# Attention and soft MoE in one kernel: V loaded as 32 keys per partition and turned by VectorE, weights in 8 KB rows with all experts on chip, second layer in four column groups

## The chip, the cores and the metric

The kernel runs on one core of one Trainium2 chip. The metric is device time in microseconds (us). The span of a profiled execution differs from the timed median by a few us (239.4 against 235.39 for the kernel before); stages are read from the span. The runs of a kernel spread over about 3% here, and comparisons use the fast runs. The profiled execution of the kernel before was one of its slower ones: the spans of its fast runs in later calls are 232.2 to 237.4 us. So a difference of some 3 us between its stages and those of another profile says little.

The views of the profile name the engines: PE is TensorE's matmuls, PEld its weight loads, DVE is VectorE, ACT is ScalarE, POOL is GpSimd, and SP issues DMAs. "L294" is line 294 of the kernel. The granted clock is the share of TensorE's full clock that it was allowed, 1.00 at most. The chain is the work that ended last, followed back step by step to what released it.

## The reference

Eight batches of eight heads, 576 queries and keys each, head size 64; 16 "beacon" keys per head come first and are visible to every query, the 576 others are causal. The attention output is the input `x` (4608 x 512) of a soft mixture of experts with 8 experts of 4 slots.

```python
k_all = concatenate([beacon_k, k], axis=2)            # 16 + 576 keys
v_all = concatenate([beacon_v, v], axis=2)
scores = where(causal, -1e9, q @ k_all.T / 8)
attn = softmax(scores) @ v_all                        # B,H,S,D -> x: (B*S, H*D)
logits = x @ phi                                      # 4608 x 32
slot_input = softmax(logits, axis=0).T @ x            # 32 x 512
h = relu(slot_input[e] @ w1[e]); slot_out[e] = h @ w2[e]   # 512x1024, 1024x512
out = softmax(logits, axis=1) @ slot_out
```

## The kernel before

The kernel works through 32 pairs of heads, four pairs per batch. `n` is the pair, `g = n % 4` its place in the batch. In each pair TensorE computes scores of pair `n`, transposes q and k of pair `n + 1`, and multiplies the exponentials of pair `n - 1` with V. A batch's routing (transposes of `x`, logits, their transposes `dT`, slot inputs) is spread as pieces of work over the next batch's pairs. In the timelines below each engine takes its own instructions in program order.

V is read as rows of 64 float32 (256 bytes), one key per partition, and cast by GpSimd and VectorE:

```python
    def load_v(b, part):
        for c in ((0, 1), (2,), (3,), (4,))[part]:
            vf[(b, c)] = vfp.tile([P, H, D], FP, name="vf", tag="vf")
            if c == 0:
                nc.sync.dma_start(out=vf[(b, c)][0:Nb], in_=beacon_v[b].rearrange("h n d -> n h d"))
            lo, hi = max(0, c * P - Nb), min(S, (c + 1) * P - Nb)
            p0 = lo + Nb - c * P
            nc.sync.dma_start(out=vf[(b, c)][p0:p0 + hi - lo],
                              in_=v[b, :, lo:hi, :].rearrange("h p d -> p h d"))
# ... cut ...
    def cast_v(b, c):
        kn = P if c < 4 else UL
        (nc.vector if c % 2 else nc.gpsimd).tensor_copy(out=vh[b % 2][0:kn, c, :, 0:D], in_=vf[(b, c)][0:kn])
```

The slot inputs of a batch need the transposed logits `dT`, which VectorE copies out of PSUM, the memory that TensorE writes to:

```python
    def dt_piece(b):
        # ... cut: five TensorE transposes of eLh into tp ...
        nc.vector.tensor_copy(out=dT[b][:, 0:4, :], in_=tp[:, 0:4, :])
        nc.vector.tensor_copy(out=dT[b][0:UL, 4, :], in_=tp[0:UL, 4, :])
        nc.vector.memset(dT[b][0:Nb, 0, :], 0.0)
    # si_piece(b): TensorE multiplies x with dT[b]
    for n in range(NP + 1):                       # the loop over pairs, shortened
        score(n, 0); (0, 2, 3, 2)[n % 4] pieces of routing work; score(n, 1)
        transp(n + 1); attend(n - 1, 0); score(n, 2); attend(n - 1, 1); score(n, 3)
        load_pair(n + 5); load_v(b + 1, g); cast_v(...); now and then load_w(...)
```

In the third pair of a batch (g = 2) the work is the last transpose and both logits pieces; in the fourth (g = 3) it is `dt_piece` and `si_piece`. The experts' weights are cast to float16 by GpSimd's DMA in 1 MB pieces (source rows of 4 KB for w1 and 2 KB for w2) into six rotating buffers per matrix; experts 6 and 7 wait until a buffer is free. The MoE stage then runs, expert by expert:

```python
        nc.scalar.activation(hTz[:, e, :, e * SPE:(e + 1) * SPE], hp[:, :, :], AF.Relu)
        for t in range(NFC):                                         # 8 matmuls, one after the other
            nc.tensor.matmul(sop[0:NSL, :], hTz[:, e, t, :], w2h[e][:, t * Dm:(t + 1) * Dm],
                             start=(e == 0 and t == 0), stop=(e == E - 1 and t == NFC - 1))
```

The softmax here doesn't subtract the row's maximum and nothing guards it: scores larger than these inputs give would overflow.

## Time and profile before

| | us |
|---|---|
| Median of the 3 runs | 235.39 (235.05 to 239.95) |
| Profiled span | 239.4 |
| Routing sums begin (end of attention and its routing) | 180.24 |
| Routing sums and MoE stage, to the scaling of the slot outputs | 30.96 (180.24 to 211.20) |
| Output stage | 28.2 (211.20 to 239.4) |

From the page of the kernel before: busy time and its share of the span with the number of instructions, then the busy tenths in 40 slices of 6 us. PEclk is the clock that TensorE was granted, in tenths.

```profile
PE 187.1 (78%) x3512; PEld 129.1 (54%) x3512; DVE 130.8 (55%) x304; ACT 127.4 (53%) x187; POOL 89.4 (37%) x161
...
PE   0579778869986898797898698899869999979800
...
PEclk9999889985999799999999979689996569995555
DMA  6999999999899899999999999272599999919995
...
q1 hardware_dynamic: 50880, 38.35, 56.3%
q0 software_dynamic: 12800, 16.78, 41.5%
```

DMA is full in attention and again while the last weights come in. The two last lines are the DMA queues: packets, MB written, share of 16 engines. Of q1, the records of single packets give 54.0 us of all 16 engines to packets of 256 bytes, nearly all of them V.

Busy time by window, kernel before: window, its length, busy us of PE, PEld, DVE, ACT and POOL with instruction counts, granted clock, DMA share (over 1 where packets overlap), GB/s written.

```profile
100.00:120.00 20.00, 17.48 (x419) 13.00 (x417) 14.53 (x35) 14.74 (x22) 10.79 (x18) 1.00 1.17 262
180.00:190.00 10.00, 9.43 (x124) 5.15 (x121) 1.35 (x7) 0.40 (x2) 4.30 (x6) 0.59 1.18 205
```

TensorE is busy 17.48 of 20 us in attention, with DMA saturated as well. In the MoE stage it runs at a granted clock of 0.59, while the DMA engines are full with the last experts' weights.

The timeline of one fourth pair of the kernel before (start, duration, engine, line, what; in brackets idle time before and its releaser):

```profile
108.35 0.49 DVE L237 TENSOR_TENSOR xb_141<-av_153,r_2528 128x320 f16<-128x320 f32 x1
...
109.07 0.23 DVE L285 COPY dT<-tr 128x128 f16<-128x128 f16 x1 [0.23 <-PE tr L283]
...
109.35 0.07 DVE L287 MEMSET dT<- 16x16 uint32 x1
109.48 0.67 PE L294 MATMUL tr<-dT,xb_142 128*128 128x32 f16 x20 [0.45 <-DVE dT L287]
```

VectorE finishes the third pair at 108.84 and is free when the logits' transposes arrive; TensorE loses 0.45 us before the slot inputs (L294).

The second layer before, two experts of the chain of work that ended last (start, duration, what):

```profile
187.56 3.59 PE av_152 L397 x8
...
196.97 1.90 PE av_152 L397 x8
```

### The profile page before, as it was taken

Reading aid. Unit: us, or ns where it says so; the run is one execution under the profiler, and the core shown is the slowest. Engines: PE = TensorE matmul, PEld = TensorE weight load, DVE = VectorE, ACT = ScalarE, POOL = GpSimd, SP = SyncE. Lnnn points to the kernel's source line nnn. Section 1 sums busy time; section 2 is a strip of 40 time slices with the busy share of each in tenths; the row PEclk is TensorE's granted clock in tenths of the full one; section 3 lists DMA queues with packets and bytes.
Section 4 is the critical chain, followed back from the end, with each engine's and each line's share of the span. In section 5 each row is a group of like instructions: output and inputs, shape, how many; then the busy total and the mean of one; then the engine's idle time right before and its main releaser. Section 6 shows DMA issues by size and latency. Waiting matters only on the chain.

```text
span 239.4 us, 8048 instructions
## 1 busy us (share of the span) xinstructions
PE 187.1 (78%) x3512; PEld 129.1 (54%) x3512; DVE 130.8 (55%) x304; ACT 127.4 (53%) x187; POOL 89.4 (37%) x161
## 2 busy tenths in 40 slices
PE   0579778869986898797898698899869999979800
PEld 0457566647664766575666476677646445532200
DVE  4583967555777566777667666566652000058800
ACT  2075576747767487776786758477710000057700
POOL 4080645442652732744645363443542420000000
PEclk9999889985999799999999979689996569995555
DMA  6999999999899899999999999272599999919995
GB/s 193 225 300 281 317 225 243 298 258 240 220 248 228 193 230 282 205 273 263 258 317 262 230 201 277 43 127 41 92 161 202 209 206 210 159 81 422 416 413 248
DMA packets 63715, 55.63 MB, mean 232 GB/s; under 512 B 41920, under 2 KB 50112, under 8 KB 62656
## 3 DMA queue, kind: packets, MB, share of 16 engines
q1 hardware_dynamic: 50880, 38.35, 56.3%
q0 software_dynamic: 12800, 16.78, 41.5%
q8 instruction: 27, 0.44, 0.8%
q14 instruction: 8, 0.07, 0.1%
HBM read 62.46 MB, written 9.44 MB: 300 GB/s over the span
## 4 chain that ended last, share of the span: by engine, by line
PE 47%; DMA 16%; ACT 13%; DVE 5%; SPq 5%; POOL 5%; issue 4%; ACTq 0%
DMA vf<-in_v_dram 14%; ACT ex L208 10%; PE av_152 L397 8%; PE sc_156 L202 6%; PE av_152 L229 6%; PE tr L187 6%; PE fp L413 5%; PE tr L256 3%; DVE xT L261 3%; PE tr L392 3%; PE sc_157 L202 3%; SPq L103 3%; PE tr L271 2%; PE av_153 L229 2%; DMA kf<-in_k_dram 2%
## 5 line engine op out<-in xcount | busy, mean ns | idle before, releaser
L208 ACT ACTIVATE ex<-sc_156 128x1024 f16<-128x1024 f32 x64 | 63.0, 984 | 47.4 <-PE sc_156 L202 47.2
L208 ACT ACTIVATE ex<-sc_157 128x992 f16<-128x992 f32 x64 | 48.0, 751 | 12.2 <-PE sc_157 L202 12.1
L210 POOL TENSOR_SCALAR_AFFINE_SELECT ex<-ex 128x1024 f16<-128x1024 f16 x32 | 34.9, 1092 | 46.9 <-ACT ex L208 46.9
L229 PEld LDWEIGHTS <-ex 128*128 128x128 f16 (+2 forms) x960 | 40.6, 113 | 12.8 <-issue 10.9
L397 PE MATMUL av_152<-w2h,hTz 128*32 128x512 f16 x64 | 20.1, 471 | 2.3 <-ACT hTz L395 2.3
L187 PE MATMUL tr<-idb,kf 64*64 64x64 bf16 x576 | 16.6, 204 | 2.0 <-issue 0.8
L261 DVE COPY xT<-tr 128x1024 f16<-128x1024 f16 x16 | 10.5, 687 | 13.2 <-PE tr L256 13.2
L187 PEld LDWEIGHTS <-qf 64*64 64x64 bf16 x576 | 13.4, 118 | 7.4 <-issue 6.2
L187 PE MATMUL tr<-idb,qf 64*64 64x64 bf16 x576 | 16.8, 205 | 0.6 <-DMA qf<-in_q_dram 0.5
L395 ACT ACTIVATE hTz<-tr 128x32 f16<-128x32 f32 x8 | 1.6, 198 | 28.8 <-PE tr L392 28.8
L401 DVE TENSOR_SCALAR soh<-av_152,rd 32x512 f16<-32x512 f32 x1 | 0.7, 737 | 29.0 <-PE av_152 L397 29.0
L187 PEld LDWEIGHTS <-kf 64*64 64x64 bf16 x576 | 14.3, 119 | 2.9 <-issue 2.6
L413 PE MATMUL fp<-soh,eLh 32*128 32x512 f16 x36 | 14.1, 522 | 1.4 <-DVE soh L401 0.8
L415 ACT ACTIVATE osb<-fp,rc 128x512 f32<-128x512 f32 x18 | 11.8, 687 | 5.9 <-PE fp L413 5.6
L202 PE MATMUL sc_156<-qT_129,kT_132 64*128 64x128 bf16 (+1 forms) x110 | 9.6, 276 | 6.9 <-POOL kT_132 L192 4.8
L243 POOL CAST vh_138<-vf 128x512 f16<-128x512 f32 (+1 forms) x12 | 7.7, 639 | 19.0 <-DMA vf<-in_v_dram 19.0
L216 POOL TENSOR_SCALAR_AFFINE_SELECT ex<-ex 80x160 f16<-80x160 f16 x32 | 10.6, 331 | 10.7 <-ACT ex L208 10.3
L202 PEld LDWEIGHTS <-kT_132 64*128 64x128 bf16 (+1 forms) x198 | 8.6, 110 | 11.1 <-POOL kT_132 L192 5.7
L417 DVE TENSOR_SCALAR osb<-fp,rc 128x512 f32<-128x512 f32 x18 | 13.1, 748 | 2.4 <-PE fp L413 1.6
L120 POOL DMA_DIRECT2D w1h<-in_moe_w_dram x16 | 11.5, 724 | 6.6 <-PE tr L392 6.6
L120 POOL DMA_DIRECT2D w2h<-in_moe_w_dram x16 | 12.1, 758 | 4.4 <-PE av_152 L397 4.4
L229 PE MATMUL av_153<-vh_138,ex 128*128 128x65 f16 (+2 forms) x240 | 11.5, 202 | 2.1 <-issue 2.1
(206 smaller groups left out, 318.9 us busy)
## 6 DMA issues: line engine op xcount, KB each, us to landing
qf<-in_q_dram SPq DMA_DIRECT2D x32, 288.0 KB, 6.2
kf<-in_k_dram SPq DMA_DIRECT2D x32, 288.0 KB, 6.3
w1h<-in_moe_w_dram POOLq DMA_DIRECT2D x16, 512.0 KB, 8.6
w2h<-in_moe_w_dram POOLq DMA_DIRECT2D x16, 512.0 KB, 8.9
out_dram<-osb SPq DMA_DIRECT2D x8, 1024.0 KB, 8.2
vf<-in_v_dram SPq DMA_DIRECT2D x24, 256.0 KB, 7.0
vf<-in_v_dram SPq DMA_DIRECT2D x8, 224.0 KB, 6.9
vf<-in_v_dram SPq DMA_DIRECT2D x8, 160.0 KB, 7.2
```

The lines of the kernel that those rows point to most:

```text
L120: nc.gpsimd.dma_start(out=d[e][:, o:o + 2048].rearrange("p (c f) -> p c f", c=c), in_=src)
L187: nc.tensor.transpose(tp[po:po + 64, j, :], hi, idb[po:po + 64, po:po + 64])
L202: nc.tensor.matmul(sc[0:kn, a, col:col + un], kT[n % 3][64 * a:64 * a + 64, P * c:P * c + kn], qT[n % 3][64 * a:64 * a + 64, u0:u0 + un], ...
L208: nc.scalar.activation(ex[n][:, :, o:o + w], sc[:, :, 0:w], AF.Exp, scale=scale)
L210: nc.gpsimd.affine_select(out=ex[n][:, :, 0:512].rearrange("p a (c t) -> p a c t", c=4), in_=ex[n][:, :, 0:512].rearrange("p a (c t) -> p ...
L216: nc.gpsimd.affine_select(out=ex[n][0:UL, :, o:o + UL], in_=ex[n][0:UL, :, o:o + UL], compare_op=AL.is_ge, fill=0.0, base=0, pattern=[[0, ...
L229: nc.tensor.matmul(avs[a][0:m, i * DD:(i + 1) * DD], ex[n][0:kn, a, o:o + m], vh[b % 2][0:kn, c, h, :], start=(c == 0), stop=(c == i))
L261: nc.vector.tensor_copy(out=xT[b][:, :, P * cs[0]:P * cs[0] + 2 * P].rearrange("p t (i u) -> p i t u", i=2), in_=tp[:, :, :, :])
L397: nc.tensor.matmul(sop[0:NSL, :], hTz[:, e, t, :], w2h[e][:, t * Dm:(t + 1) * Dm], start=(e == 0 and t == 0), stop=(e == E - 1 and t == NF ...
L413: nc.tensor.matmul(fp_[:, :], etok(cg, j), soh[:, :], start=True, stop=True)
L415: nc.scalar.activation(osb[:, j, :], fp_[:, :], AF.Copy, scale=rc[:, i:i + 1])
L417: nc.vector.tensor_scalar(out=osb[:, j, :], in0=fp_[:, :], scalar1=rc[:, i:i + 1], scalar2=None, op0=AL.mult)
```

## The change

Its intent: fewer and larger DMA packets, so that DMA no longer limits attention; no casts of V; the MoE stage without waits for weights and with a shorter second layer. Space for all experts is found by lending the last two experts' place to the q, k and V buffers during attention. The core of the diff, with cuts marked by dots and three comments put in for cut code:

```diff
+    TK = 32
...
+        # 32 keys of one head on a partition (8 KB source row), cast to float16 by GpSimd's DMA
+            nc.gpsimd.dma_start(
+                out=main[32 * qd:32 * qd + 32, :],
+                in_=bass.AP(tensor=v.tensor, offset=v.offset + b * H * S * D + lo,
+                            ap=[[S * D, H], [4 * TK * D, 4], [1, TK * D]]))
...
+        # rest(m): keys 496 to 575, one row per head
+        for what in (((0, 1), (16,)), ((2, 3), ()), ((), (17, 18)), ((), ()))[part]:
+            for x in what:
+                (block if x < 16 else rest)(x)
+    def turn_v(b, tail):
+        src = vtile(b, tail).bitcast(FP).rearrange("p (j e) -> p e j", j=TK)
+        dst = vh[b % 2].bitcast(FP)
+        if tail:
+            nc.vector.transpose(
+                out=dst[0:96, 0:4].rearrange("p c h e -> p e (c h)")[:, 0:D // 2], in_=src[0:96])
+        else:
+            nc.vector.transpose(
+                out=dst[:, 1:NCH].rearrange("p c h e -> p e h c")[:, 0:D // 2], in_=src)
...
+    # beacon_v_in(b): beacon rows by GpSimd's DMA into vh, after the transposes
...
-            src = moe_w1[e, r * 256:(r + 1) * 256].rearrange("(c p) f -> p c f", p=P)
+            src = moe_w1[e, r * 256:(r + 1) * 256].rearrange("(p r) f -> p (r f)", r=2)
...
-        nc.gpsimd.tensor_copy(out=kT[n % 3][:, 0:Nb], in_=bkT[:, n, :])
+        nc.vector.tensor_copy(out=kT[n % 3][:, 0:Nb], in_=bkT[:, n, :])
...
             if b + 1 < B:
                 load_v(b + 1, g)
-                for c in ((), (0, 1), (2,), (3, 4))[g]:
-                    cast_v(b + 1, c)
+                if g == 2:
+                    turn_v(b + 1, 1)
+                    turn_v(b + 1, 0)
+                if g == 3:
+                    beacon_v_in(b + 1)
-            if n % 3 != 2 and n >= 3 and wl < 24:
+            want = 23 * (n + 1) // 28 if n < 28 else (25, 28, 30, 32)[n - 28]
+            while wl < want:
...
+            z = 32 * (t % 4)
+            nc.tensor.matmul(sop[z:z + NSL, :], hTz[:, e, t, :], w2c(e, t),
+                             start=(e == 0 and t < 4), stop=(e == E - 1 and t >= 4))
+    for e in range(E + 1):
+        if e < E:
+            first_layer(e)
+        if e > 0:
+            second_layer(e - 1)
```

Cut: the layouts of first-layer weights (read with a step of four elements) and slot inputs that go with it, and the fourfold copy of routing weights and logits, so that the last matmul adds the four groups.

More of the change, by code (lines that the diff above doesn't have):

```diff
@@ L46 @@
     DD = D + 1
+    DP = D + 2
     scale = 1.0 / D ** 0.5
@@ L70 @@
     const = ctx.enter_context(tc.tile_pool(name="const", bufs=1))
-    qkp = ctx.enter_context(tc.tile_pool(name="qkp", bufs=5))
-    vfp = ctx.enter_context(tc.tile_pool(name="vfp", bufs=6))
     exq = ctx.enter_context(tc.tile_pool(name="exq", bufs=2))
     sml = ctx.enter_context(tc.tile_pool(name="sml", bufs=4))
-    wh = ctx.enter_context(tc.tile_pool(name="wh", bufs=6))
+    arena = const.tile([P, E * 8192], F16, name="arena")
+    lend = (E - 2) * 8192
     sc_scope = ExitStack()
@@ L82 @@
     qf, kf = {}, {}
+    QKS = 5
     def load_pair(n):
         b, g = divmod(n, H // 2)
-        for (d, src, nm) in ((qf, q, "qf"), (kf, k, "kf")):
-            t = qkp.tile([P, J, D], FP, name=nm, tag=nm)
+        for i, (d, src) in enumerate(((qf, q), (kf, k))):
+            o = lend + (2 * (n % QKS) + i) * 2 * J * D
+            t = arena[:, o:o + 2 * J * D].bitcast(FP).rearrange("p (j d) -> p j d", j=J)
             nc.sync.dma_start(
-                out=t[:, :, :],
+                out=t,
                 in_=src[b, 2 * g:2 * g + 2].rearrange("h s d -> (h s) d").rearrange(
@@ L92, in load_pair @@
             d[n] = t
-    vf = {}
-    def load_v(b, part):
-        for c in ((0, 1), (2,), (3,), (4,))[part]:
-            vf[(b, c)] = vfp.tile([P, H, D], FP, name="vf", tag="vf")
-            if c == 0:
-                nc.sync.dma_start(out=vf[(b, c)][0:Nb], in_=beacon_v[b].rearrange("h n d -> n h d"))
-            lo, hi = max(0, c * P - Nb), min(S, (c + 1) * P - Nb)
-            p0 = lo + Nb - c * P
-            nc.sync.dma_start(out=vf[(b, c)][p0:p0 + hi - lo],
-                              in_=v[b, :, lo:hi, :].rearrange("h p d -> p h d"))
+    TK = 32
@@ new lines, with vtile, block, rest @@
+    vend = lend + 2 * QKS * 2 * J * D
+    vmore = const.tile([P, 2, TK * D], F16, name="vmore")
+    def vtile(b, tail):
+        if b % 2 == 0:
+            return vmore[:, tail, :]
+        return arena[:, vend + tail * TK * D:vend + (tail + 1) * TK * D]
+    vrows = v.rearrange("b h s d -> (b h) (s d)")
+    vall = v.rearrange("b h s d -> (b h s d)")
+    vh = [const.tile([P, NCH, H, DP], F16, name=f"vh{i}") for i in range(2)]
+    def load_v(b, part):
+        main, tail = vtile(b, 0), vtile(b, 1)
+        def block(qd):
+            lo = (32 * qd - Nb) * D
+            if b == 0 and qd == 0:
+                nc.gpsimd.dma_start(out=main[0:1, Nb * D:TK * D], in_=vrows[0:1, 0:(TK - Nb) * D])
+                nc.gpsimd.dma_start(
+                    out=main[1:4, :],
+                    in_=bass.AP(tensor=v.tensor, offset=v.offset + lo + 4 * TK * D,
+                                ap=[[4 * TK * D, 3], [1, TK * D]]))
+                nc.gpsimd.dma_start(
+                    out=main[4:32, :],
+                    in_=bass.AP(tensor=v.tensor, offset=v.offset + S * D + lo,
+                                ap=[[S * D, H - 1], [4 * TK * D, 4], [1, TK * D]]))
+                return
+            nc.gpsimd.dma_start(
+                out=main[32 * qd:32 * qd + 32, :],
+                in_=bass.AP(tensor=v.tensor, offset=v.offset + b * H * S * D + lo,
+                            ap=[[S * D, H], [4 * TK * D, 4], [1, TK * D]]))
+        def rest(m):
+            lo = (TK * m - Nb) * D
+            w = min(TK * D, S * D - lo)
+            p0 = 32 * (m - 16)
+            nc.gpsimd.dma_start(out=tail[p0:p0 + H, 0:w],
+                                in_=vrows[b * H:(b + 1) * H, lo:lo + w])
+        for what in (((0, 1), (16,)), ((2, 3), ()), ((), (17, 18)), ((), ()))[part]:
+            for x in what:
+                (block if x < 16 else rest)(x)
@@ new lines, in turn_v, with beacon_v_in @@
+    def turn_v(b, tail):
[3 more added lines that the diff above has]
+            nc.vector.transpose(
+                out=dst[0:96, 0:4].rearrange("p c h e -> p e (c h)")[:, 0:D // 2],
+                in_=src[0:96])
+        else:
+            nc.vector.transpose(
+                out=dst[:, 1:NCH].rearrange("p c h e -> p e h c")[:, 0:D // 2], in_=src)
+    def beacon_v_in(b):
+        nc.gpsimd.dma_start(out=vh[b % 2][0:Nb, 1, :, 0:D],
+                            in_=beacon_v[b].rearrange("h n d -> n h d"))
@@ L106 @@
     NPC = 4 * E
-    w1h, w2h = {}, {}
+    WP = 2048
+    wloc = [m * WP for m in range(24)] + [lend + WP * x for x in (3, 4, 5, 6, 7, 0, 1, 2)]
     def load_w(m):
         e, r = divmod(m, 4)
-        d, nm = (w1h, "w1h") if r < 2 else (w2h, "w2h")
-        if r % 2 == 0:
-            d[e] = wh.tile([P, 4096], F16, name=nm, tag=nm)
-        o = (r % 2) * 2048
         if r < 2:
-            src = moe_w1[e, r * 256:(r + 1) * 256].rearrange("(c p) f -> p c f", p=P)
+            src = moe_w1[e, r * 256:(r + 1) * 256].rearrange("(p r) f -> p (r f)", r=2)
@@ L117, in load_w, with w1c @@
         else:
-            src = moe_w2[e, (r - 2) * 512:(r - 1) * 512].rearrange("(c p) f -> p c f", p=P)
-        c = src.shape[1]
-        nc.gpsimd.dma_start(
-            out=d[e][:, o:o + 2048].rearrange("p (c f) -> p c f", c=c), in_=src)
+            src = moe_w2[e, (r - 2) * 512:(r - 1) * 512].rearrange("(p r) d -> p (r d)", r=4)
+        nc.gpsimd.dma_start(out=arena[:, wloc[m]:wloc[m] + WP], in_=src)
+    def w1c(e, c, t):
+        o = wloc[4 * e + c // 2] + (c % 2) * F + (t // 4) * 512
+        return arena[:, o:o + 512].rearrange("p (f r) -> p f r", r=4)[:, :, t % 4]
@@ L123, with w2c @@
+    def w2c(e, t):
+        o = wloc[4 * e + 2 + t // 4] + (t % 4) * Dm
+        return arena[:, o:o + Dm]
     load_pair(0)
@@ L126 @@
     load_pair(1)
-    for part in range(4):
-        load_v(0, part)
     phif = const.tile([P, NDC, NSL], FP, name="phif")
@@ L133 @@
     load_pair(4)
+    nc.vector.memset(vtile(0, 0)[0:1, 0:Nb * D], 0.0)
+    nc.vector.memset(vtile(0, 1), 0.0)
+    for part in range(4):
+        load_v(0, part)
+    nc.vector.memset(vtile(1, 1), 0.0)
     idb = const.tile([P, P], BF, name="idb")
@@ L145 @@
         nc.vector.memset(qT[i][:, 0:Nb], 0.0)
-    vh = [const.tile([P, NCH, H, DD], F16, name=f"vh{i}") for i in range(2)]
     for i in range(2):
@@ L149 @@
     xb = [const.tile([P, NCH, H, D], F16, name=f"xb{i}") for i in range(2)]
-    eLh = const.tile([NSL, Nb + N], F16, name="eLh")
+    eLh = const.tile([P, Nb + N], F16, name="eLh")
     nc.vector.memset(eLh[:, 0:Nb], 0.0)
-    dsum9 = const.tile([NSL, 2 * B], FP, name="dsum9")
+    dsum9 = const.tile([P, 2 * B], FP, name="dsum9")
     siacc = const.tile([P, NDC, NSL], FP, name="siacc")
     nc.vector.memset(siacc[:, :, :], 0.0)
-    hTz = const.tile([P, E, NFC, NSL], F16, name="hTz")
-    nc.gpsimd.memset(hTz[:, :, :, :], 0.0)
-    phih = const.tile([P, NDC, NSL], F16, name="phih")
+    phih = const.tile([P, NDC, 4, NSL], F16, name="phih")
     bkT = const.tile([P, NP, Nb], BF, name="bkT")
@@ L231, in attend @@
                     ex[n][0:kn, a, o:o + m],
-                    vh[b % 2][0:kn, c, h, :],
+                    vh[b % 2][0:kn, (c + 1) % NCH, h, 0:DD],
                     start=(c == 0), stop=(c == i))
@@ L239, in attend @@
             in1=r5[:, :].unsqueeze(2).broadcast_to([P, NCH, D]), op=AL.mult)
-    def cast_v(b, c):
-        kn = P if c < 4 else UL
-        (nc.vector if c % 2 else nc.gpsimd).tensor_copy(out=vh[b % 2][0:kn, c, :, 0:D], in_=vf[(b, c)][0:kn])
     xT = {}
@@ L270, in logit_piece @@
         for t in range(NDC):
-            nc.tensor.matmul(lp[0:NSL, 0:w], phih[:, t, :],
+            nc.tensor.matmul(lp[:, 0:w], phih[:, t, :, :].rearrange("p g s -> p (g s)"),
                              xT[b][:, t, Nb + hf * w:Nb + (hf + 1) * w],
@@ L274, in logit_piece @@
         o = Nb + b * S + hf * w
-        nc.scalar.activation(eLh[:, o:o + w], lp[0:NSL, 0:w], AF.Exp,
+        nc.scalar.activation(eLh[:, o:o + w], lp[:, 0:w], AF.Exp,
                              accum_out=dsum9[:, 2 * b + hf:2 * b + hf + 1])
@@ L282, in dt_piece @@
             m = P if i < 4 else UL
-            nc.tensor.transpose(tp[0:m, i, :], eLh[:, b * S + P * i:b * S + P * i + m],
+            nc.tensor.transpose(tp[0:m, i, :], eLh[0:NSL, b * S + P * i:b * S + P * i + m],
                                 idh[0:NSL, 0:NSL])
@@ L295, in si_piece @@
                     sp[:, t, :],
-                    xb[b % 2][0:m, i, 2 * t:2 * t + 2, :].rearrange("p h d -> p (h d)"),
+                    xb[b % 2][0:m, i, 4 * (t // 2):4 * (t // 2) + 4, :].rearrange(
+                        "p h d -> p (h d)").rearrange("p (f r) -> p f r", r=2)[:, :, t % 2],
                     dT[b][0:m, i, :], start=(i == 0), stop=(i == NCH - 1))
@@ L323 @@
         if n == 0:
-            for c in range(NCH):
-                cast_v(0, c)
-            nc.vector.tensor_copy(out=phih[:, :, :], in_=phif[:, :, :])
+            turn_v(0, 1)
+            turn_v(0, 0)
+            beacon_v_in(0)
+            nc.vector.tensor_copy(out=phih[:, :, :, :],
+                                  in_=phif[:, :, :].unsqueeze(2).broadcast_to([P, NDC, 4, NSL]))
         if n >= 1:
@@ L345 @@
                 load_v(b + 1, g)
-                for c in ((), (0, 1), (2,), (3, 4))[g]:
-                    cast_v(b + 1, c)
-            if n % 3 != 2 and n >= 3 and wl < 24:
+                if g == 2:
[5 more added lines that the diff above has]
+            while wl < want:
                 load_w(wl)
                 wl += 1
-    dsum = const.tile([NSL, 1], FP, name="dsum")
-    rd = const.tile([NSL, 1], FP, name="rd")
+    hTz = exq.tile([P, E, NFC, NSL], F16, name="hTz", tag="ex")
+    nc.gpsimd.memset(hTz[:, :, :, :], 0.0)
+    dsum = const.tile([P, 1], FP, name="dsum")
+    rd = const.tile([P, 1], FP, name="rd")
     nc.vector.reduce_sum(out=dsum[:, :], in_=dsum9[:, :], axis=mybir.AxisListType.X)
@@ L372 @@
             i = cg * G + j
-            nc.tensor.matmul(csp[:, i:i + 1], etok(cg, j), ones[0:NSL, :],
+            nc.tensor.matmul(csp[:, i:i + 1], etok(cg, j)[0:NSL], ones[0:NSL, :],
                              start=True, stop=True)
@@ L380, with first_layer @@
     sop = avs[0]
-    while wl < min(NPC, 24):
-        load_w(wl)
-        wl += 1
-    for e in range(E):
-        while wl < min(NPC, 4 * (e + 6)):
-            load_w(wl)
-            wl += 1
+    def first_layer(e):
         hp = ps_tr.tile([P, NFC, SPE], FP, name="tr", tag="tr")
@@ L391, with second_layer @@
             for c in range(NDC):
-                nc.tensor.matmul(hp[:, t, :], w1h[e][:, c * F + t * P:c * F + (t + 1) * P],
-                                 siT[:, c, e * SPE:(e + 1) * SPE],
+                nc.tensor.matmul(hp[:, t, :], w1c(e, c, t), siT[:, c, e * SPE:(e + 1) * SPE],
                                  start=(c == 0), stop=(c == NDC - 1))
         nc.scalar.activation(hTz[:, e, :, e * SPE:(e + 1) * SPE], hp[:, :, :], AF.Relu)
+    def second_layer(e):
         for t in range(NFC):
-            nc.tensor.matmul(sop[0:NSL, :], hTz[:, e, t, :],
-                             w2h[e][:, t * Dm:(t + 1) * Dm],
-                             start=(e == 0 and t == 0), stop=(e == E - 1 and t == NFC - 1))
-    soh = const.tile([NSL, Dm], F16, name="soh")
-    nc.vector.tensor_scalar(out=soh[:, :], in0=sop[0:NSL, :], scalar1=rd[:, 0:1],
+            z = 32 * (t % 4)
[6 more added lines that the diff above has]
+            second_layer(e - 1)
+    soh = const.tile([P, Dm], F16, name="soh")
+    nc.vector.tensor_scalar(out=soh[:, :], in0=sop[:, :], scalar1=rd[:, 0:1],
                             scalar2=None, op0=AL.mult)
@@ L407 @@
     for cg in range(NG):
-        osb = wh.tile([P, G, Dm], FP, name="osb", tag="w1h")
+        osb = arena[:, cg * 4096:(cg + 1) * 4096].bitcast(FP).rearrange("p (j d) -> p j d", j=G)
         dst = out[cg * P * G:(cg + 1) * P * G, :].rearrange("(p j) d -> p j d", j=G)
```

## The prediction

> **What bounds the kernel now.** Three stages, read from the busy times by window and the chain of waits (profiled span 239.4 us).
>
> 1. Attention, 15 to 173 us, 32 head pairs. PE is busy 16 to 17.5 of each 20 us, DMA is saturated (share 0.96 to 1.17). The undisturbed stretch from 99.9 to 118.9 us takes 19.05 us per batch of four pairs; the average is about 20.5. So waits for V (the chain gives 14% to "DMA vf") cost only about 11 us in all. By packet records, V's 256-byte packets take 54 us of all 16 engines, the weights 99.
> 2. MoE, 181.5 to 211.2 us = 29.7 us: first layer 0.93 us per expert, an idle wait for the ReLU, then eight second-layer matmuls, 3.6 us at the halved clock (four experts) or 1.9 us (four).
> 3. Output, 28 us, DMA at over 400 GB/s; unchanged.
>
> **What the change moves.**
>
> - V: 8 KB source rows. Weight packets (2048 source bytes 98 ns, 4096 bytes 172 ns) extrapolate to an estimated 320 ns for 8192: V falls from 54 to about 23 us of DMA time, weights from 99 to about 82. DMA stops being the limit of attention. Worth at most 11 us.
> - VectorE gains two transposes per batch of 1024 four-byte elements. The SBUF cast of 512 float32 took 0.51 to 0.57 us, so an estimated 1.1 us each, and loses two casts.
> - These transposes stand in VectorE's order directly before the dT copies for which TensorE waits in the next pair. Their last two V pieces are issued by GpSimd only in the same pair. Laid over today's timeline: GpSimd would be free at 107.2, two issues of 0.7 us end at 108.6; the Trainium skill ("DMA: Bandwidth & Descriptors", anatomy of one DMA) gives about 2 us fixed cost. VectorE arrives at 108.9, so it waits about 2 us, then transposes for 2.2. TensorE's slot-input matmuls, now at 109.5, would start at about 113: 3.5 to 4.5 us of idle TensorE per batch, seven times = 25 to 31 us, plus some re-throttled clock after each gap, 3 to 8 us.
> - Start: the identity matrix is made after nine GpSimd DMA issues, and batch 0's beacon DMA waits for the transposes: first attention-times-V about 3 us later than 17.6.
> - MoE: four column groups. The skill ("TensorE: Matmul & The Clock Gate", packing small matmuls) gives 2.4 times for three groups, which no run here shows yet. Estimated second layer 0.6 to 1.2 us per expert. The first layer, with stride-4 weights, at most 1.15 us (the stride-4 loads of eLh ran at 36 ns each against 29). The ReLU wait is hidden. Estimated stage 13 to 18 us instead of 29.7: about -14.
>
> **Sum.** Attention -11 + 20 to 35, start +3, MoE -14: from about -2 to +13. I lean to the low side since the stall depends on landing times I cannot see: **240 us, 8 in 10 between 225 and 253; faster by over 2% 0.29, within 2% 0.28, slower 0.43.**
>
> **What would show it.** Right: VectorE waiting for V DMA before the large transposes, once per batch; TensorE idle before the slot-input matmuls on the dT memset or copies; V packets of 8 KB source; DMA share under 1 in attention; MoE about 15 us. Wrong: batches of 19 us without such a gap; MoE still near 30 us; transposes far from 1.1 us.
>
> **What would make it wrong.** If the last V pieces land before VectorE arrives, the stall shrinks to about 2 us per batch and the kernel lands near 225. If strided weight loads or mode switches are slow, MoE gains less.

## The result, and the profile after

| | before | after |
|---|---|---|
| Median, us | 237.67 (4 runs) | 280.14 (4 runs, 278.44 to 281.52) |
| Profiled span, us | 239.4 | 279.5 |
| Routing sums begin, us | 180.24 | 233.15 |
| Routing sums and MoE stage, us | 30.96 | 18.19 (to 251.34) |
| Output stage, us | 28.2 | 28.2 |
| Ratio of fast runs | | 1.1906 (95%: 1.1769 to 1.2044) |

A ratio is the mean time of one kernel's fast runs over that of the other's fast runs of the same rounds, so it is not quite the ratio of the medians quoted. The change makes the kernel 19% slower. MoE gains 12.8 us; attention loses 52.9 us.

From the page of the kernel after, the same lines:

```profile
PE 179.5 (64%) x3512; PEld 129.3 (46%) x3512; DVE 156.8 (56%) x339; ACT 127.4 (46%) x187; POOL 100.5 (36%) x171
...
PE   0647639719941997099619950995099878998800
...
PEclk9999958968985589569957995799558996556985
DMA  7997949937993399469927991699347996005997
```

TensorE now has a hole in every batch, its clock falls to half around each, and DMA, which was to be relieved, swings between full and idle.

Waits of the kernel after (engine and line, for whom; total us, times, longest):

```profile
PE tr L342 <- DVE dT L335: 52.4, 8, 9.5
DVE vh L145 <- DMA arena<-in_v_dram: 18.0, 4, 5.1
DVE vh L145 <- DMA vmore<-in_v_dram: 12.7, 3, 5.4
PE av L282 <- DMA vh<-in_beacon_v_dram: 4.5, 1, 4.5
```

The timeline of the same spot, kernel after, in another batch:

```profile
108.14 1.06 POOL L134 DMA_DIRECT2D vmore<-in_v_dram  x2
...
109.34 0.49 DVE L290 TENSOR_TENSOR xb<-av,r 128x320 f16<-128x320 f32 x1
...
114.08 2.02 DVE L145 STREAM_TRANSPOSE vh<-vmore 96x1024 f32<-96x1024 f32 x1 [4.24 <-DMA vmore<-in_v_dram]
116.13 2.06 DVE L149 STREAM_TRANSPOSE vh<-vmore 128x1024 f32<-128x1024 f32 x1
118.05 0.20 DVE L333 COPY dT<-tr 128x128 f16<-128x128 f16 x1
...
118.44 0.71 PE L342 MATMUL tr<-dT,xb 128*128 128x32 f16 x20 [8.43 <-DVE dT L335]
```

Read from above: GpSimd issues the last two V pieces at 108.14. VectorE arrives at about 109.8, waits 4.24 us, transposes for 4.1 us, and only then copies the `dT` for which TensorE has stood still 8.43 us. TensorE does nothing else in the hole: its next instruction in program order is the one that waits.

The price in clock and what DMA does meanwhile, busy time by window around an earlier hole, kernel after (columns as before):

```profile
70.00:80.00 10.00, 9.21 (x196) 6.76 (x196) 7.25 (x18) 7.23 (x12) 7.74 (x14) 1.00 1.02 235
80.00:90.00 10.00, 1.00 (x27) 0.80 (x27) 4.74 (x6) 1.57 (x3) 1.12 (x2) 0.61 0.68 162
90.00:100.00 10.00, 9.82 (x181) 7.63 (x178) 5.70 (x15) 5.54 (x7) 4.42 (x8) 0.54 0.48 126
```

After the hole TensorE is busy 9.82 of 10 us for 181 matmuls, where 196 had taken 9.21 us, at a granted clock of 0.54 instead of 1.00.

The second layer after, two pieces of the chain:

```profile
238.79 0.97 PE av L450 x8
239.76 1.16 PE tr L443 x32
```

Eight second-layer matmuls take 0.97 us instead of 3.59, both at about half clock, and the ReLU wait between the layers is gone.

### The profile page after: what moved, and what is told of

Its sections match the earlier page's. It is cut to its first block, busy times and chain, and to the rows that moved or that the text cites. A ratio compares the mean times of both kernels' runs of the same rounds, so it can differ in the third digit from the quotient of the medians.

```text
span 279.5 us, 8018 instructions
## 1 busy us (share of the span) xinstructions
PE 179.5 (64%) x3512; PEld 129.3 (46%) x3512; DVE 156.8 (56%) x339; ACT 127.4 (46%) x187; POOL 100.5 (36%) x171
## 4 chain that ended last, share of the span: by engine, by line
PE 37%; DVE 22%; DMA 15%; ACT 14%; POOL 5%; issue 2%; ACTq 0%; DVEq 0%; POOLq 0%
ACT ex L261 12%; PE av L282 9%; PE sc L255 9%; DMA arena<-in_v_dram 6%; PE tr L240 6%; DVE vh L149 6%; DMA vmore<-in_v_dram 6%; DVE vh L145 5%; DVE xT L309 4%; DVE arena L475 3%; PE tr L443 3%; PE av L450 3%; DMA arena<-in_moe_w_dram 2%; ACT eLh L323 2%; PE tr L342 2%
## 5 line engine op out<-in xcount | busy, mean ns | idle before, releaser
L261 ACT ACTIVATE ex<-sc 128x1024 f16<-128x1024 f32 (+3 forms) x128 | 107.1, 869 | 112.5 <-PE sc L255 112.3
L255 PE MATMUL sc<-qT,kT 64*128 64x128 bf16 (+5 forms) x576 | 50.7, 275 | 14.8 <-ACT ex L261 7.0
L282 PE MATMUL av<-vh,ex 128*128 128x65 f16 (+2 forms) x960 | 50.1, 211 | 5.0 <-DMA vh<-in_beacon_v_dram 4.5
L282 PEld LDWEIGHTS <-ex 128*128 128x128 f16 (+2 forms) x960 | 42.5, 117 | 15.2 <-issue 13.3
L342 PE MATMUL tr<-dT,xb 128*128 128x32 f16 (+1 forms) x160 | 5.7, 187 | 52.4 <-DVE dT L335 52.4
L242 DVE COPY qT<-tr 128x576 bf16<-128x576 bf16 x32 | 24.2, 756 | 26.1 <-PE tr L240 26.1
L255 PEld LDWEIGHTS <-kT 64*128 64x128 bf16 (+1 forms) x576 | 22.0, 108 | 25.8 <-issue 12.7
L290 DVE TENSOR_TENSOR xb<-av,r 128x320 f16<-128x320 f32 x64 | 31.4, 491 | 2.2
L240 PE MATMUL tr<-idb,arena 64*64 64x64 bf16 x1152 | 31.8, 212 | 1.3 <-DVE bkT L227 0.4
L240 PEld LDWEIGHTS <-arena 64*64 64x64 bf16 x1152 | 27.5, 126 | 9.6 <-issue 8.7
L242 DVE COPY kT<-tr 128x576 bf16<-128x576 bf16 x32 | 23.9, 746 | 0.1
L166 POOL DMA_DIRECT2D arena<-in_moe_w_dram x32 | 18.2, 568 | 0.3 <-issue 0.3
L145 DVE STREAM_TRANSPOSE vh<-vmore 96x1024 f32<-96x1024 f32 x4 | 8.1, 2024 | 12.7 <-DMA vmore<-in_v_dram 12.7
L475 DVE TENSOR_SCALAR arena<-fp,rc 128x512 f32<-128x512 f32 x18 | 12.7, 747 | 1.5 <-PE fp L471 1.1
```

The source lines that it names most:

```text
L145: nc.vector.transpose(out=dst[0:96, 0:4].rearrange("p c h e -> p e (c h)")[:, 0:D // 2], in_=src[0:96])
L166: nc.gpsimd.dma_start(out=arena[:, wloc[m]:wloc[m] + WP], in_=src)
L240: nc.tensor.transpose(tp[po:po + 64, j, :], hi, idb[po:po + 64, po:po + 64])
L242: nc.vector.tensor_copy(out=dst[:, Nb:Nb + S].rearrange("p (s j) -> p s j", j=J), in_=tp[:, :, :].rearrange("p j s -> p s j"))
L255: nc.tensor.matmul(sc[0:kn, a, col:col + un], kT[n % 3][64 * a:64 * a + 64, P * c:P * c + kn], qT[n % 3][64 * a:64 * a + 64, u0:u0 + un], ...
L261: nc.scalar.activation(ex[n][:, :, o:o + w], sc[:, :, 0:w], AF.Exp, scale=scale)
```

## The experiments

Theory A: VectorE, executing in order, stands at the transposes until V pieces issued in the same pair have landed, then transposes for 4 us, while TensorE waits for `dT`. Rivals: the V transfers themselves are slow or DMA is short (B); clock, GpSimd issues or DMA are causes of their own (C); the paced weights and lent buffers cost attention (D). Times are medians; the medians of the kernel before in the same calls lay between 237.06 and 238.52 us for all timed pairs below.

### v_early: the last V pieces one pair earlier

```diff
-        for what in (((0, 1), (16,)), ((2, 3), ()), ((), (17, 18)), ((), ()))[part]:
+        for what in (((0, 1), (16,)), ((2, 3), (17, 18)), ((), ()), ((), ()))[part]:
```

> Only change to the changed kernel: the last two V pieces of a batch are issued one pair earlier, beside the third and fourth block. Theory A (VectorE, in order, sits on the transposes until the pieces issued in the same pair land, 30.7 us over seven batches in the profile after): VectorE's wait for V falls under 6 us, TensorE's idle time before the slot-input matmuls from 52 us to 25 to 30 us (the two transposes of 2.04 us each stay in the way), time 245 to 256 us. Rival B (the V transfers with 8 KB rows are slow in themselves or DMA is short, so the wait moves to another piece): wait stays above 20 us, time above 270 us.

Measured: 258.91 us, correct, ratio to the kernel before 1.0868. VectorE's wait for V is 7.6 us in all (4.4 and 3.2), TensorE's gap before the slot inputs 33.3 us. Both lie a little above what was expected, and so does the time, but the order of size is that of A, and B is out: the wait does not move elsewhere. What is left of the gap is mostly the transposes themselves (seven times 4.1 us are 28.7).

```profile
PE tr L342 <- DVE dT L335: 33.3, 8, 6.4
```

### late_turn: the transposes one pair later, after the dT copies

```diff
+        if g == 3 and b + 1 < B:
+            turn_v(b + 1, 1)
+            turn_v(b + 1, 0)
         if n + 1 < NP:
             transp(n + 1)
...
-                if g == 2:
-                    turn_v(b + 1, 1)
-                    turn_v(b + 1, 0)
```

> Loads as in the changed kernel, but the two transposes stand one pair later in VectorE's order: after the dT copies and before the copies of q and k. Theory A: the pieces have landed by then (wait under 4 us in all), and about 1 us of the 4.1 us per batch hides while TensorE transposes q; TensorE's gap of 52 us before the slot-input matmuls goes to under 5 us, a new one of about 3 us per batch stands at the scores or the transposes of q and k; time 238 to 252 us. Rival B: no better than v_early by more than noise because 4.1 us of VectorE per batch cost the same wherever they stand.

Measured: 259.33 us, correct, ratio 1.0926: no better than v_early, as the rival said. The gap before the slot inputs fell to 3.6 us, but 31.4 us of waits of the next scores for VectorE took its place. VectorE still waited 16.8 us for V where under 4 were expected, and the time lies above the expected range: a miss for A in this run. It does not show that the place is indifferent: the wait for V is 9.2 us longer than in v_early, so place and wait changed together. A later place without a wait was not run here; fixed2_place below tests the place alone.

### no_turn: no transposes after batch 0 (wrong result)

```diff
                 if g == 2:
-                    turn_v(b + 1, 1)
-                    turn_v(b + 1, 0)
+                    pass
```

(The second V buffer is filled once with a constant.)

> Wrong result on purpose: all V transfers stay, but only batch 0 is transposed; the other batches use what lies in the tiles. Shows what the transposes and their wait cost together. Theory A: TensorE's gaps before the slot-input matmuls fall from 52 us to under 5 us, the clock is granted near full in attention, time 212 to 226 us. Rival C (the throttled clock, the DMA or the GpSimd issues are a cause of their own): above 235 us.

Measured: 218.78 us, result wrong as intended, ratio 0.9192. From its page:

```profile
PE 165.1 (77%) x3512; PEld 118.0 (55%) x3512; DVE 130.8 (61%) x326; ACT 126.9 (59%) x187; POOL 100.4 (47%) x171
...
PEclk9999999999999999999999999999999855579955
DMA  6998699999999999999999999999999900069996
```

The gap before the slot inputs, as long as in the kernel before (3.6 us there too):

```profile
PE tr L342 <- DVE dT L335: 3.6, 8, 0.4
```

All V and weight transfers and all GpSimd issues are still there, so rival C as a cause of its own falls. It also splits the loss. Against this run the profile after is 65.2 us longer (279.5 - 214.3). The gaps before the slot inputs account for 48.8 us of that (52.4 - 3.6), and the same 3512 matmuls are busy 14.4 us longer (179.5 - 165.1), which is the lower clock after the holes. Both together are 63.2 us. A batch of four pairs takes 18.15 us here (five periods between the copies of `x`'s transposes at 57.42 and 148.17 us), 20.5 before and 28.0 after. DMA is as full here as in the kernel before (share 1.05 against 1.07 between 60 and 140 us), so the runs do not show that DMA stopped limiting attention.

### undo_v: V as before, the rest of the change kept

The edit puts `load_v` and `cast_v` of the kernel before in place of the new V path, and nothing else. Its core:

```diff
-                if g == 2:
-                    turn_v(b + 1, 1)
-                    turn_v(b + 1, 0)
-                if g == 3:
-                    beacon_v_in(b + 1)
+                for c in ((), (0, 1), (2,), (3, 4))[g]:
+                    cast_v(b + 1, c)
```

> The changed kernel with the V path of the kernel before (256-byte rows, casts on GpSimd and VectorE), all else kept: 8 KB weight rows, all experts on chip, column groups. Theory A (the V path alone makes the change slow, the rest gains about 13 us in the MoE stage): time 218 to 229 us, MoE stage about 17 us against 29.7. Rival D (the paced weights or the lent buffers cost attention too): above 235 us.

Measured: 233.05 us, correct, ratio 0.9813 (0.9741 to 0.9884): less gain than expected. The MoE stage is as short as in the change, but attention ends later (first-layer loads begin at 186.2 us against 181.5 before), and GpSimd waits 70.2 us for V (28.5 before).

```profile
POOL vh L247 <- DMA vf<-in_v_dram: 70.2, 18, 7.3
```

So rival D has a part here. The likely reason is that all 32 weight pieces now move during attention, beside 256-byte V packets that already filled the DMA engines; pacing and lent buffers were not tested apart. The V path is what makes the change slow; without it the rest gains about 2%.

### m_turn: what a transpose costs

A row of VectorE transposes of scratch data at the end of the kernel before, with other engines idle.

```diff
+    for _ in range(3):
+        nc.vector.transpose(out=c3, in_=a3)     # packed in, packed out
+    for _ in range(3):
+        nc.vector.transpose(out=c3, in_=as3)    # step of 128 bytes in, packed out
+    for _ in range(3):
+        nc.vector.transpose(out=o4, in_=a3)     # packed in, the kernel's step out
+    for _ in range(3):
+        nc.vector.transpose(out=o4, in_=as3)    # both, as the kernel does
```

> The kernel before with a row of VectorE transposes of scratch data at its very end, when GpSimd and the other engines are idle; only their durations matter. In the changed kernel one transpose of 1024 four-byte elements took 2.04 us, not the 1.1 us forecast. Theory W (a four-byte element takes two passes whatever the layout): 1024 float32 with packed input and output still 2.0 to 2.1 us, half of it 1.0 to 1.1 us, 1024 float16 about 1.1 us, 2048 float16 about 2.1 to 2.2 us. Rival S (the strides of input or output cost the time): packed float32 about 1.1 us, and one of the strided forms 2 us. Rival G (GpSimd in the way): all forms 1.1 us here.

Groups of its profile (busy us, mean ns of one, idle before), in the order strided out, strided both, strided in, packed, packed 1024 float16, and last a plain copy with the strided input:

```profile
L444 DVE STREAM_TRANSPOSE tbw<-taw 128x1024 f32<-128x1024 f32 x3 | 6.0, 1997 | 0.1
L446 DVE STREAM_TRANSPOSE tbw<-taw 128x1024 f32<-128x1024 f32 x3 | 6.2, 2064 | 0.1
L442 DVE STREAM_TRANSPOSE tcw<-taw 128x1024 f32<-128x1024 f32 x3 | 5.7, 1905 | 0.1
L440 DVE STREAM_TRANSPOSE tcw<-taw 128x1024 f32<-128x1024 f32 x3 | 3.7, 1245 | 0.1
L448 DVE STREAM_TRANSPOSE tcw<-taw 128x1024 f16<-128x1024 f16 x3 | 3.7, 1232 | 0.1
L452 DVE COPY tcw<-taw 128x1024 f32<-128x1024 f32 x3 | 3.1, 1032 | 0.1
```

Rival S wins, and G is out, since both steps cost 2.06 us with GpSimd idle too. Packed, 1024 four-byte elements take 1.245 us, as long as two-byte ones (1.232). A step on either side makes it 1.9 to 2.0 us, on both 2.06. A plain copy with the same strided input took 1.03 us, so on the input side it is the transpose that minds the step, not VectorE's reads as such; a copy with a strided output was not run. The forecast of 1.1 us was taken from packed casts: the transpose itself adds about 0.15 us to it, the steps another 0.8.

### colgroups: the column groups alone

```diff
-            nc.tensor.matmul(sop[0:NSL, :], hTz[:, e, t, :],
+            z = 32 * (t % 4)
+            nc.tensor.matmul(sop[z:z + NSL, :], hTz[:, e, t, :],
```

(with the fourfold routing weights and logits; all else as before)

> The kernel before with one part of the change alone: the second layer in four column groups (and the fourfold copy of the routing weights and logits that it needs). ReLU wait, weight layout, DMA and V as before. If the groups run side by side, eight second-layer matmuls take about 1.0 us at half clock (as in the profile after, 0.97) instead of 3.6 or 1.9: the MoE stage falls from about 30 to 17 to 22 us, unless the last experts' weights, which wait for freed buffers, now arrive too late. Time 222 to 232 us. Rival (the weights' DMA limits that stage): 232 us or more with TensorE waiting for weights.

Measured: 238.69 us, correct, ratio 1.0021 (0.9933 to 1.0110): no gain, the rival's case. Its timeline shows where the gain goes; experts 5 and 6 of 0 to 7:

```profile
191.67 1.04 PE L399 MATMUL av<-w2h,hTz 128*32 128x512 f16 x8 [0.29 <-ACT hTz L396]
192.65 1.01 PE L393 MATMUL tr<-siT,w1h 128*128 128x4 f16 x32
194.47 0.62 PE L399 MATMUL av<-w2h,hTz 128*32 128x512 f16 x4 [0.80 <-DMA w2h<-in_moe_w_dram]
196.97 0.62 PE L399 MATMUL av<-w2h,hTz 128*32 128x512 f16 x4 [1.89 <-DMA w2h<-in_moe_w_dram]
```

The first six experts take 2.3 us each; then TensorE waits for the weights of the last two, which can only be loaded once buffers are free, and from the first first-layer load to the end of the second layer the stage takes 28.7 us (179.04 to 207.79), against 29.7 before. Here the groups bring nothing while the last weights come late.

### undo_vc: V as before and one group, weights on chip

The edit puts one group back into undo_v:

```diff
-            nc.tensor.matmul(sop[z:z + NSL, :], hTz[:, e, t, :], w2c(e, t),
-                             start=(e == 0 and t < 4), stop=(e == E - 1 and t >= 4))
+            nc.tensor.matmul(sop[0:NSL, :], hTz[:, e, t, :], w2c(e, t),
+                             start=(e == 0 and t == 0), stop=(e == E - 1 and t == NFC - 1))
```

> undo_v (V as before, the rest of the change kept) with the second layer in one group again: what is left of the change is 8 KB weight rows, all experts on chip, the layers overlapped by one expert. If the column groups gain only together with weights on chip, eight second-layer matmuls take 3.4 us at half clock or 1.7 to 1.9 at full, the MoE stage 24 to 36 us instead of 17, so 6 to 18 us slower than undo_v (233): 238 to 250 us. Rival (on-chip weights alone give the gain of undo_v): within 3 us of undo_v.

Measured: 245.69 us, correct, ratio 1.0344. First and second layer together take 27.1 us (first load at 188.5, slot outputs scaled at 215.65), against 17.0 in undo_v (186.2 to 203.18). The groups are worth 10 us of this stage when weights are there. In the two layers, 29.7 us before, the groups alone gain 1.0 us, the weights on chip (with the two layers overlapped) alone 2.6, both together 12.7. In the whole kernel neither half gains alone: undo_vc loses, because attention ends 7 us later than before.

### fixed_v: a version from these results

Loads a batch ahead; the last 80 keys by 256-byte cast DMA straight into `vh` (one transpose less per batch); beacon rows put into the V block before it is turned; the remaining transpose in two halves, at `g == 2` and at the next `g == 0`, each after the routing work and before the copies of q and k; the identity before the first V loads. Its core:

```diff
+    def load_beacon(b):
+        nc.gpsimd.dma_start(out=vmain[0:32:4, b % 2, 0:Nb * D],
+                            in_=beacon_v[b].rearrange("h n d -> h (n d)"))
+    def load_tail(b):
+        nc.gpsimd.dma_start(out=vh[b % 2][0:UL, 0, :, 0:D],
+                            in_=v[b, :, 4 * P - Nb:S, :].rearrange("h p d -> p h d"))
+    def turn_half(b, hf):
+        e0 = hf * (D // 4)
+        src = vmain[:, b % 2, :].bitcast(FP).rearrange("p (j e) -> p e j", j=TK)
+        dst = vh[b % 2].bitcast(FP)[:, 1:NCH].rearrange("p c h e -> p e h c")
+        nc.vector.transpose(out=dst[:, e0:e0 + D // 4], in_=src[:, e0:e0 + D // 4])
...
+        if g == 2 and b + 1 < B:
+            turn_half(b + 1, 0)
+        if g == 0 and 0 < b < B:
+            turn_half(b, 1)
         if n + 1 < NP:
             transp(n + 1)
...
+            if b + 2 < B and g > 0:
+                for qd in ((0, 1), (2, 3), ())[g - 1]:
+                    load_block(b + 2, qd)
+                if g == 3:
+                    load_beacon(b + 2)
+            if b + 1 < B and g == 2:
+                load_tail(b + 1)
```

> A version made from what the runs say: V blocks are loaded a whole batch ahead; the last 80 keys go by cast DMA straight to where they are used, so the second transpose of each batch is gone; beacon rows go into the block before the transpose; the remaining transpose is cut in two halves of about 1 us, each placed where VectorE otherwise waits for TensorE's q transposes; identity made before the first V loads. Theory A: no wait of VectorE for V, no TensorE gap over 1 us, about 18.5 us per batch of four pairs as in the run without transposes, time 214 to 224 us, faster than every kernel so far. Rival B (V by 8 KB rows through GpSimd's queue cannot keep up): DMA waits come back, above 232 us.

Measured: 246.48 us, correct, ratio 1.04: a miss. VectorE waited 32.3 us for beacon rows, by the author's reading those of the other half of the buffer, which the waiting transpose does not read. The next run tests that reading.

### fixed2: the same with two tiles for the two V buffers

```diff
-    vmain = const.tile([P, 2, TK * D], F16, name="vmain")
+    vmain = [const.tile([P, TK * D], F16, name=f"vmain{i}") for i in range(2)]
```

> fixed_v with one edit: the two V buffers are two tiles instead of two halves of one. In fixed_v VectorE waited 32 us for the beacon rows of the other half, a wait that the program's dependency tracking added, since it counts a write with a partition step as touching the whole tile; the instruction list shows that wait gone. Theory A: VectorE's wait for V or beacon rows under 4 us in all, no TensorE gap over 1 us before scores or slot inputs, 18 to 18.8 us per batch of four pairs, time 214 to 224 us (before 237). Rival B (the 8 KB V path cannot keep up whatever its order): above 230 us, with DMA waits elsewhere.

Measured: 213.04 us, correct, ratio 0.9026 (0.8969 to 0.9083), the fastest of all. VectorE waits 5.7 us in all for V (in two places) where it had waited 32.3, so the wait in fixed_v was one of the program's bookkeeping and not of the data. The 5.7 us are a little over the expected 4; a batch takes 18.3 us, as expected. TensorE's gap before the slot inputs is 3.6 us. From its page:

```profile
PE 167.2 (79%) x3512; PEld 119.4 (57%) x3512; DVE 137.9 (65%) x336; ACT 127.1 (60%) x187; POOL 93.9 (44%) x155
...
PEclk9999999999999999999999999999999855579955
```

The timeline of fixed2 around one half of the transpose:

```profile
95.10 1.23 PE L296 MATMUL tr<-xT,phih 128*128 128x288 f16 x8
...
95.55 1.13 DVE L132 STREAM_TRANSPOSE vh<-vmain 128x512 f32<-128x512 f32 x1
...
97.11 0.76 DVE L219 COPY qT<-tr 128x576 bf16<-128x576 bf16 x1 [0.44 <-PE tr L217]
```

The 1.13 us pass while TensorE computes logits and transposes q; VectorE is still 0.44 us early for the copy. Rival B falls for good: V in 8 KB rows, loaded a batch ahead, keeps up. Because several things were changed at once, this run shows what they do together, not what each is worth.

### fixed2_place: only the place of the transpose put back

```diff
-        if g == 2 and b + 1 < B:
-            turn_half(b + 1, 0)
-        if g == 0 and 0 < b < B:
-            turn_half(b, 1)
...
                 load_tail(b + 1)
+                turn_half(b + 1, 0)
+                turn_half(b + 1, 1)
```

> fixed2 with one edit: both halves of the transpose stand where the change had its transposes, at the end of the third pair, right before the dT copies; data long there. If the place alone matters: TensorE idle before the slot-input matmuls 1.5 to 2.2 us per batch, 10 to 16 us in all, some more by a lower clock after the gaps, time 222 to 236 us against 213. Rival (with 2.3 us instead of 4.1 and no DMA wait VectorE catches up): within 3 us of fixed2.

Measured: 228.3 us, correct, ratio 0.9651. The gap before the slot inputs is 13.5 us instead of 3.6, and TensorE's busy time 173.0 us instead of 167.2: the place costs 9.9 us in gaps and 5.8 us in clock, together 15.7, against 15.3 us between the medians. So place does matter once a block is short enough to fit where there is slack.

```profile
PE tr L319 <- DVE dT L312: 13.5, 8, 2.3
PEclk9999979979996999799799969988999955559965
```

Each of the six holes of 2.1 to 2.3 us (they end at 46.6, 67.2, 87.8, 108.4, 129.1 and 150.0 us) is followed by a dip of the granted clock (slices of 5.6 us); fixed2, without these holes, has no dip in attention.

### w_held and w_none: why the pieces land late

w_held issues no weights in the second pair of a batch, w_none none before the last four pairs.

```diff
-            while wl < want:
+            while wl < want and (g != 1 or n >= 28):
```
```diff
-            want = 23 * (n + 1) // 28 if n < 28 else (25, 28, 30, 32)[n - 28]
+            want = 0 if n < 28 else (25, 28, 30, 32)[n - 28]
```

> The changed kernel with one edit: no weight piece is issued in the second pair of a batch, the pair before the last two V pieces; it follows in the third and fourth. Theory Q (the last V pieces wait behind the megabyte of weights issued one pair earlier on the same queue, and behind other full-rate transfers): their landing falls from 5 to 6 us to 3 to 4.5 us, VectorE's wait for V from 30.7 us in all to 12 to 22, time 262 to 272 us. Rival F (8 rows on few engines and the completion take 5 us by themselves): wait stays within 4 us of 30.7, time 277 us or more.

> The changed kernel with no weight piece at all before the last four pairs; the 32 pieces all follow there, so the time is not of interest (the weights then arrive late), only the wait of VectorE for V in attention. If what is left of the wait in w_held (22.1 us of 30.7) is traffic of weights issued in other pairs: landing of the last V pieces 2.5 to 3.5 us, wait 5 to 12 us in all. Rival F (the pieces are slow by themselves, or q and k are what they wait behind): wait above 16 us.

Measured: w_held 271.3 us, ratio 1.1461, wait for V 22.1 us; w_none 314.1 us in one run of unknown state (late weights, as foreseen), wait 15.2 us; both correct. The DMA issues of the last V pieces in the kernel after (KB each, median us from issue to landing):

```profile
vmore<-in_v_dram POOLq DMA_DIRECT2D x8, 32.0 KB, 5.6
...
vmore<-in_v_dram POOLq DMA_DIRECT2D x4, 16.0 KB, 5.9
```

And the same lines of w_none:

```profile
vmore<-in_v_dram POOLq DMA_DIRECT2D x8, 32.0 KB, 4.0
...
vmore<-in_v_dram POOLq DMA_DIRECT2D x4, 16.0 KB, 3.7
```

(The rows of 32 KB also count the piece that is issued earlier.) Without the weight piece of the pair before, which stands in front of the V pieces on GpSimd's queue, the 30.7 us of wait fall by 8.6; without any weights in attention by 15.5, and 15.2 remain, 2.2 us per batch (one run of unknown state). The second expectation was missed on the high side, so the weights are not the whole story, and "slow by themselves" is not either. How much of the rest is fixed cost, and how much the q and k traffic, stays open. w_held met its expected time (262 to 272 us) and just missed its expected wait (12 to 22 us).

## Why the prediction was wrong

The time was outside the stated range (280 against 225 to 253), and "faster" or "within 2%" were given too much weight. The mechanism was named and was right: transposes in front of the `dT` copies, waiting for V pieces of the same pair, once per batch. What failed is the cost of the stall: the landing of the last V pieces, counted as 2 us, and the two transposes, counted as 2.2 us; from both followed idle time and clock that were too small. The prediction's own list of what would show it wrong names "transposes far from 1.1 us", and that sign came (2.04 us each). Term by term:

- **"VectorE ... waits about 2 us".** Measured 4.4 us per batch (30.7 over seven). The Trainium skill ("DMA: Bandwidth & Descriptors", anatomy of one DMA) gives a fixed cost of about 2 us plus bytes over the rate; the pieces took 5.6 to 5.9 us from issue to landing. The same page (two DMAs through the same engine are not ordered) says that within one queue of one DMA engine descriptors start in order. The first was used and the second left out of the sum, though the diff shows the weight piece in front; by w_held that piece is worth 8.6 of the 30.7 us. That w_none waits 2.2 us per batch, near the 2 of the prediction, is luck: its pieces took 3.7 to 4.0 us to land.
- **"then transposes for 2.2".** Measured 4.1. The estimate came from packed casts; m_turn gives 1.245 us for a packed transpose and 2.06 for one with the steps as used.
- **"25 to 31 us" of idle TensorE.** Measured 48.8 us over the floor of 3.6, which follows from the two terms above: 7 x (4.4 + 4.1) = 59 us of VectorE, less the part that passes while TensorE is still at work.
- **"some re-throttled clock ..., 3 to 8 us".** Measured 14.4 us more busy time for the same matmuls. The skill ("TensorE: Matmul & The Clock Gate", part 1) has the clock halved after an idle window of about 3.4 us; a hole of 8 us spans one, and the windows above show it: 0.61 and 0.54 after 1.00. But fixed2_place shows the clock fall after holes of 2.1 to 2.3 us too, so staying under 3.4 us was not enough here. The underestimated holes carried this term with them.
- **"Attention -11".** The stretch taken as undisturbed was not: 18.15 us per batch in no_turn against 20.5 is about 2.4 us, over seven batches 16 us (some 3 us of it may be the slower profiled run of the kernel before; no_turn also has no casts of V). A miss in the other direction.
- **MoE "13 to 18 us ... about -14".** 18.19 instead of 30.96 us with the routing sums, -12.8. Right in size. But the column groups alone bring next to nothing (colgroups), and 10 us with weights on chip.
- **Start "about 3 us later than 17.6".** 22.44, so 4.8 us; TensorE waited 4.5 us for the first beacon rows.

The measured terms roughly close: -16 + 48.8 + 14.4 + 4.8 - 12.8 is 39 us, against 40.1 between the profiled spans.

There is also a slip in the sum: its terms of 25 to 31 and 3 to 8 us add up to 28 to 39, but "20 to 35" was entered. With 28 to 39 the sum would have been +6 to +17 us, a centre near 247. "I lean to the low side since the stall depends on landing times I cannot see" pulled the same way. Even the right sum ends at +17, so the sizes, not only the slip and the leaning, were at fault.

## What to carry to other kernels

Taking work off DMA can lengthen a kernel if it puts a block of several us, or a wait for fresh data, into the order of an engine that another engine needs at that moment: load a batch ahead, cut the block to the slack that the timeline shows, and place it there. Cost a transpose with strides by a transpose with those strides, and count what stands in front of a small transfer on its queue. Two changes to one stage (on-chip weights, column groups) can be worth 2.6 and 1.0 us of it apart and 12.7 together, so test them together too.

## What the Trainium skill lacked or had wrong

- "Vector Engine (DVE) Microarchitecture Reference", 3.8: says the 32x32 transpose is pipelined to sustain one element per cycle per lane. Section 3.8 says nothing of steps. Packed, 1024 elements took 1.245 us; with a step on one side 1.9 to 2.0 us, on both 2.06. Section 5.2 of that page gives costs of stepping every element, measured on other operations, and none for the transpose; a copy with a strided input paid nothing here (1.03 us).
- "DMA: Bandwidth & Descriptors", anatomy of one DMA: the formula of 2 us plus bytes over rate has no term for what else is on the queue and the engines. Pieces of 16 KB took 5.6 to 5.9 us from issue to landing with paced 1 MB weight pieces, and 3.4 to 3.7 us without weights.
- "TensorE: Matmul & The Clock Gate", part 1: a whole idle window of about 3.4 us was not needed here; the clock fell after each of six holes of 2.1 to 2.3 us (fixed2_place).
- The same page, part 3: gives 2.38 times for three column groups, and no figure for four. Four groups here did eight matmuls of 512 columns in 0.97 us against 3.59, both at about half clock, 3.7 times.
- The same page lists when the fast weight load is on, by column step, but no cost for the step. 32 first-layer loads with their small matmuls took 1.16 us with a step of four elements, 0.96 packed, both at about half clock.
